# Attention scores in full-array or quarter-array matmuls: changing how one fused attention and gated-MLP kernel makes its scores

## Chip, cores and metric

The kernel runs on one core of one Trainium2 chip. The metric is the device time of one execution in microseconds (us); the median over the runs is compared.

## The reference, cut to what is computed

`q`, `k`, `v` are float32 of shape (8 batches, 8 heads, 576 tokens, 64); `w_in` is (512, 2048), `w_out` (2048, 512). Keys and values are first averaged over groups of 8 tokens, so that each head has 72 keys.

```python
k_p = k.reshape(B, H, Sp, pool, D).mean(axis=3)          # Sp = 72, D = 64
v_p = v.reshape(B, H, Sp, pool, D).mean(axis=3)
scores = scale * np.matmul(q, k_p.transpose(0, 1, 3, 2))
scores = scores - np.max(scores, axis=-1, keepdims=True)
attn = np.exp(scores)
attn = attn / (np.sum(attn, axis=-1, keepdims=True) + 1e-09)
out = np.matmul(attn, v_p)                                # then heads side by side: x (4608, 512)
h = x @ w_in
g = h * np.clip(h + 3.0, 0.0, 6.0) / 6.0
return g @ w_out
```

## The kernel before, in words

The 4608 tokens are cut into 12 blocks (`BLOCKS`: 512, 256, then ten of 384). Blocks 0 to 3 go through the MLP one by one (`Step`: `h` is x times w_in at line 841, `out` is g times w_out at line 872). The eight others go two by two through `super_block` (products at line 1127, output products at line 1204 in `out_plain` or 1279 in `out_seven`), which saves products by sums of quarters of the matrices and streams its weights from DRAM in tiles `ws`. Almost all products are split in high and low fp32r parts; the scores and the transposes are plain float32.

Attention runs ahead of the MLP and in its gaps. Its work for a block is a list of steps (`block_steps`), and `Paced` deals the steps out over slots between groups of MLP matmuls: attention of block 2 and half of block 3 goes beside the MLP of block 1, and so on; attention for a pair of blocks goes beside the super block ahead of it, 0.85 of it (`CUTS`) beside its first products. A block has tiles of 128 tokens (three for a block of 384). Heads are kept as four pairs: `qt` holds a tile's queries as (2 heads x 64 dimensions) on 128 partitions, and `kbds` holds the pooled keys of a pair as a block diagonal, 128 x 144, with zeros off the diagonal. A group `g` is two pairs, four heads.

For one tile and group, `Scores` does the following:

- `product` (line 465): one matmul for each of the two pairs, the full 128 x 128 array, 144 columns. A tile whose 128 tokens lie in two batches (every batch boundary that falls inside a tile; from block 2 on these are the tiles at tokens 1664, 2816 and 3968) needs two per pair, added up, with the other batch's queries set to zero by a memset on POOL (line 241).
- `top` (line 469): DVE takes the maximum of each head.
- `exps` (line 474): four activations on ScalarE (ACT), each with its sum.
- `invert` (lines 491, 492) on DVE, and `divide` (lines 503, 509) on POOL from block 2 on: the main 64 columns of each head go to `a`, the last eight of each head to `ar`.

`transposes` (lines 574, 576) then turns `a` and `ar` on TensorE, ACT and DVE copy them out as high and low parts, and `av` (line 648) multiplies by the values. In `block_steps` a transpose of a group follows three (later two) score steps behind its own. PSUM banks for all this come from `att_bank`, which goes round a list of three (`a0`, `a1`, `o3`), or two while output products run.

The engines' instruction order comes from the Tile framework, apart from a window near the start, in which `ORDER` lists every engine's order by number. `plan` places the loads and preparation of keys and values of a later batch: the first `SIDE` steps ahead of their first use.

## Time and profile before

| | us |
|---|---|
| median of 3 runs | 886.65 (886.44 to 888.14) |
| the profiled execution's own time | 887.28 |
| its span, first to last instruction | 885.5 |
| PE (TensorE matmul) busy in it | 868.3 (98%) |
| DVE busy | 650.5 (73%) |
| ACT busy | 551.9 (62%) |
| POOL busy | 81.4 (9%) |

PE are matmul records, PEld the loads of stationary operands (LDWEIGHTS), DVE is VectorE, ACT ScalarE, POOL GpSimd, SP the queue that issues most DMAs. A float32 matmul of the program shows as two MATMUL records, each with its own LDWEIGHTS; a transpose and an fp32r matmul show as one. A record's duration reaches from its start to a modelled end, and successive matmuls overlap; the pace of matmuls is therefore read from the distance between starts.

### The profile page before, as it was taken

The numbers are of one execution on the slowest core, as the hardware profiler recorded it, in microseconds if no ns is written. First come the engines' busy times: TensorE is split into PE (matmuls) and PEld (weight loads), VectorE is DVE, ScalarE is ACT, GpSimd is POOL, SyncE is SP. The second block draws the span as 40 slices with busy tenths as digits, with TensorE's granted clock in tenths as the row PEclk, the third lists the DMA queues.
The fourth block names the chain that finished last, engine by engine and source line by source line (L and its number), as shares of the span: only waits on it lengthen the run. The fifth ranks groups of instructions, "written<-read, shape, count | busy, mean of one in ns | idle before, by whom it ended". The sixth has DMA issues, their size and how long they took to land.

```text
span 885.5 us, 15623 instructions
## 1 busy us (share of the span) xinstructions
PE 868.3 (98%) x5360; PEld 812.0 (92%) x5360; DVE 650.5 (73%) x1322; ACT 551.9 (62%) x1515; POOL 81.4 (9%) x168
## 2 busy tenths in 40 slices
PE   7999999999999999999999999999999999999998
PEld 7788888988989999999888999899999999999998
DVE  5887754567877885878888588987588887466664
ACT  6998766655666654887444688655576756354442
POOL 4100002110111100112000101100110200000000
PEclk9999999999999999999999999999999999999999
DMA  9970206995425254996697969877886687877784
GB/s 315 391 280 0 77 20 202 366 318 161 122 80 161 60 156 123 367 308 214 205 284 234 379 217 288 247 258 246 277 302 219 202 270 243 275 256 239 268 268 134
DMA packets 124654, 200.00 MB, mean 226 GB/s; under 512 B 13216, under 2 KB 81056, under 8 KB 124576
## 3 DMA queue, kind: packets, MB, share of 16 engines
q1 hardware_dynamic: 124432, 199.00, 68.7%
q8 instruction: 43, 0.70, 0.3%
q14 instruction: 35, 0.29, 0.1%
q10 hardware_dynamic: 144, 0.00, 0.0%
HBM read 158.08 MB, written 40.89 MB: 225 GB/s over the span
## 4 chain that ended last, share of the span: by engine, by line
PE 80%; DVE 7%; DMA 7%; ACT 3%; SPq 1%; issue 1%; DVEq 0%; ACTq 0%
PE psx L1127 21%; PE psx L1279 20%; PE pso L872 12%; PE psh L841 12%; PE psx L1204 7%; PE psa L648 4%; PE psa L465 3%; DMA wsFalse<-wd 2%; DMA stage<-q_l 2%; ACT e L474 2%; PE psa L574 1%; DMA wd<-wq 1%; DMA qt<-q_l 1%; DMA wsTrue<-wd 1%; DVE vst L385 1%
## 5 line engine op out<-in xcount | busy, mean ns | idle before, releaser
L1127 PE MATMUL psx<-x,wsFalse 128*128 128x384 f32 x768 | 150.8, 339 | 1.2 <-DMA wsFalse<-wd 1.2
L841 PE MATMUL psh<-xhi,w 128*128 128x384 f32 (+2 forms) x520 | 146.2, 340 | 0.1
L1127 PEld LDWEIGHTS psx<-x,wsFalse 128*128 128x128 f32 x768 | 132.7, 188 | 2.3 <-ACT part L1113 1.2
L1113 ACT CAST part<-g 128x768 fp32r<-128x768 f32 x100 | 83.3, 837 | 75.1 <-PE psx L1279 56.0
L872 PE MATMUL pso<-w,ghi 128*128 128x512 f32 x384 | 120.6, 399 | 0.4 <-ACT o L877 0.4
L1115 DVE TENSOR_TENSOR part<-g,part 128x768 fp32r<-128x768 f32 x100 | 95.1, 955 | 35.1 <-ACT part L1113 34.8
L1127 PE MATMUL psx<-x,wsTrue 128*128 128x384 f32 x576 | 116.1, 340 | 0.1
L1279 PE MATMUL psx<-wsFalse,part 128*128 128x256 f32 x864 | 109.6, 283 | 0.8 <-DVE g L1098 0.4
L1279 PEld LDWEIGHTS psx<-wsFalse,part 128*128 128x128 f32 x864 | 106.4, 190 | 1.6 <-ACT kept L1254 1.0
L1127 PEld LDWEIGHTS psx<-x,wsTrue 128*128 128x128 f32 x576 | 99.6, 188 | 0.8 <-DVE g L1092 0.4
L841 PEld LDWEIGHTS psh<-xhi,w 128*128 128x128 f32 x520 | 93.3, 188 | 7.5 <-DVE g L853 0.4
L474 ACT ACTIVATE e<-psa,mx 128x72 f32<-128x72 f32 x256 | 78.7, 324 | 31.4 <-DVE mx L469 29.7
L841 PE MATMUL psh<-xlo,w 128*128 128x384 f32 (+2 forms) x260 | 87.1, 336 | 0.0
L503 POOL TENSOR_TENSOR a<-e,sm 128x256 f32<-128x256 f32 x60 | 40.2, 671 | 504.4 <-DVE sm L492 414.8
L1279 PE MATMUL psx<-wsTrue,part 128*128 128x256 f32 x648 | 82.1, 283 | 0.0
L1279 PEld LDWEIGHTS psx<-wsTrue,part 128*128 128x128 f32 x648 | 79.6, 190 | 0.0
L1090 ACT ACTIVATE r<-g,small 128x384 f32<-128x384 f32 x96 | 58.5, 622 | 33.6 <-DVE g L1098 33.0
L872 PEld LDWEIGHTS pso<-w,ghi 128*128 128x128 f32 x384 | 68.9, 188 | 11.0 <-ACT o L877 0.7
L872 PE MATMUL pso<-w,glo 128*128 128x512 f32 x192 | 74.6, 399 | 0.0
L1098 DVE TENSOR_TENSOR g<-psx,c 128x384 f32<-128x384 f32 x96 | 52.0, 552 | 28.7 <-PE psx L1127 23.1
L1092 DVE SCALAR_TENSOR_TENSOR g<-r,g 128x384 f32<-128x384 f32 x96 | 54.6, 579 | 14.0 <-ACT r L1090 13.5
L1107 ACT COPY c<-psx 128x384 f32<-128x384 f32 x96 | 44.9, 485 | 23.8 <-PE psx L1127 23.7
(139 smaller groups left out, 1453.9 us busy)
## 6 DMA issues: line engine op xcount, KB each, us to landing
wsFalse<-wd SPq DMA_DIRECT2D x64, 512.0 KB, 4.8
wsTrue<-wd SPq DMA_DIRECT2D x48, 512.0 KB, 4.9
wsFalse<-w2d SPq DMA_DIRECT2D x31, 512.0 KB, 5.0
wsFalse<-w2t SPq DMA_DIRECT2D x27, 512.0 KB, 5.3
wsTrue<-w2d SPq DMA_DIRECT2D x21, 512.0 KB, 5.1
wsTrue<-w2t SPq DMA_DIRECT2D x21, 512.0 KB, 5.3
raw<-w_in_l SPq DMA_DIRECT2D x16, 512.0 KB, 8.4
raw<-w_out_l SPq DMA_DIRECT2D x16, 512.0 KB, 8.9
```

The lines of the kernel that those rows point to most:

```text
L474: nc.scalar.activation(self.e[:, h], self.ps[:, h], AF.Exp, bias=self.mx[:, h : h + 1], accum_out=self.sm[:, h : h + 1])
L841: nc.tensor.matmul(self.ps, l[f][:, c, :], r[:, c, :], start=c == 0 and i == 0, stop=c == NCC - 1 and i == 2)
L872: nc.tensor.matmul(pos, l, r, start=f == 0 and i == 0, stop=f == NF - 1 and i == 2)
L1090: nc.scalar.activation(r, src, AF.Relu, bias=half_low, scale=GSCALE / (6.0 * WSCALE))
L1092: nc.vector.scalar_tensor_tensor(out=g_of[i][:, k], in0=r, scalar=GSCALE, in1=src, op0=ALU.min, op1=ALU.mult)
L1098: nc.vector.tensor_tensor(out=g_of[i][:, k], in0=ps, in1=kept, op=ALU.add)
L1107: nc.scalar.copy(c, ps)
L1113: nc.scalar.copy(t[:, 0], src)
L1115: nc.vector.tensor_tensor(out=t[:, 1], in0=src, in1=t[:, 0].bitcast(F32), op=ALU.subtract)
L1127: nc.tensor.matmul(ps, w[:, l, c * P : (c + 1) * P], t[:, r, c], start=o in (1, 2, 5) and c == 0 and k == 0, stop=c == 1 and k == 2, skip_ ...
L1204: nc.tensor.matmul(to, l, w[:, qs, r], start=f == 0 and k == 0, stop=end and k == 2)
L1279: nc.tensor.matmul(to, t[:, l, k, i * P : (i + 1) * P], w[:, k, r], start=begin and k == 0 and y == 0 and i % 2 == 0, stop=m == NM - 1 and ...
```

## The change

From block 2 on, `TileScores` takes the place of `Scores`. For each pair of heads it issues four matmuls instead of one: head `r` of the pair lies on 64 of the partitions, and a half of the tile's tokens makes 64 columns of the stationary operand, so that each matmul uses a 64 x 64 quarter of the array, with 72 columns moving. The two heads of a pair go to different PSUM banks, the two token halves to different partitions of them. A tile's 16 matmuls stand together in program order. Since each half tile is a product of its own, a tile across two batches needs no second product and no zeros. The maxima are two instructions for a tile, as before; the exponentials come in two steps of four; add and reciprocal come once for all eight heads; the division writes in place, the tail first, so that the tile `a` is gone and `e` holds all eight heads.

The steps of a tile are now product, first exponentials, second exponentials with the division; the transposes of both groups of the tile before come behind these three, the last tile's at the block's end behind an empty step. `SIDE` goes from 12 to 16 and the preparation of values ends two steps earlier. Blocks 0 and 1 keep `Scores`; their two-batch tile writes each half's partitions alone. `ORDER` is numbered anew for the window's changed instructions (TensorE 600 to 610, DVE 186 to 181, ACT 214 to 210, POOL 25 to 21, SP 61 to 59).

```diff
-SIDE = 12
+SIDE = 16
...
     def load_q(tile):
         qtiles[tile] = []
+        t = pool.tile([P, NPAIR, P], F32, name="qt", bufs=2)
         for i, (b, s0, n, _) in enumerate(tile):
-            t = pool.tile([P, NPAIR, P], F32, name="qt", bufs=2) if i == 0 else ring("qt")
-            t = t if i == 0 else t[:, : NPAIR * P].rearrange("p (c t) -> p c t", c=NPAIR)
-            if n < P:
-                nc.gpsimd.memset(t[:, :, P // 2 :] if i == 0 else t[:, :, : P // 2], 0.0)
-            nc.sync.dma_start(t[:, :, i * (P // 2) : i * (P // 2) + n], q[b, :, :, s0 : s0 + n])
+            mine = t[:, :, i * (P // 2) : i * (P // 2) + n]
+            nc.sync.dma_start(mine, q[b, :, :, s0 : s0 + n])
             after_mark()
-            qtiles[tile].append(t)
+            qtiles[tile].append(mine)
...
         def product(self):      # Scores, blocks 0 and 1
             ps = att_bank()
-            last = len(self.tile) - 1
...
-                for r, (qt, (b, _, _, _)) in enumerate(zip(qtiles[self.tile], self.tile)):
-                    nc.tensor.matmul(to, qt[:, p, :], kbds[b % 2][:, p, :], start=r == 0, stop=r == last)
+                for r, (qt, (b, _, n, _)) in enumerate(zip(qtiles[self.tile], self.tile)):
+                    nc.tensor.matmul(
+                        to[r * (P // 2) : r * (P // 2) + n], qt[:, p, :], kbds[b % 2][:, p, :], start=True, stop=True
+                    )
...
+    class TileScores:
+        def product(self):
+            tile = self.tile
+            banks = att_bank(), att_bank()
+            self.mx, self.sm = (pool.tile([P, NG, 4], F32, name=f"{m}s", bufs=2) for m in ("mx", "sm"))
+            halves = [slice(x * D, (x + 1) * D) for x in range(2)]
+            before = last_pe() if len(window) == 2 else None
+            for p in range(NPAIR):
+                for r in (1, 0):
+                    for x, half in enumerate(halves):
+                        part = x % len(tile)
+                        b = tile[part][0]
+                        nc.tensor.matmul(
+                            banks[r][half, p * SP : (p + 1) * SP],
+                            qtiles[tile][part][halves[r], p, half if len(tile) == 1 else slice(0, D)],
+                            kbds[b % 2][halves[r], p, r * SP : (r + 1) * SP],
+                            start=True,
+                            stop=True,
+                        )
+                        if before:
+                            behind(traced[-1], before)
+                        before = traced[-1].name
+            self.ps = [x[:, : NPAIR * SP].rearrange("p (n s) -> p n s", s=SP) for x in banks]
+            self.e = pool.tile([P, NG, 4, SP], F32, name="e", bufs=2)
...
+            for r in (1, 0):
+                to = self.mx.rearrange("p g (i r) -> p (g i) r", r=2)[:, :, r]
+                nc.vector.tensor_reduce(out=to, in_=self.ps[r], axis=AX.X, op=ALU.max, negate=True)
...
+        def exps(self, g):
+            for h in range(4):
+                nc.scalar.activation(
+                    self.e[:, g, h],
+                    self.ps[h % 2][:, 2 * g + h // 2],
+                    AF.Exp,
+                    bias=self.mx[:, g, h : h + 1],
+                    accum_out=self.sm[:, g, h : h + 1],
+                )
...
+        def finish(self, engine):
+            e, sm = self.e, self.sm
+            nc.vector.tensor_scalar(out=sm, in0=sm, scalar1=1e-9, scalar2=None, op0=ALU.add)
+            nc.vector.reciprocal(sm, sm)
+            rest = rests[self.tile] = pool.tile([P, NG, 2 * REM], F32, name="ar", bufs=2)
+            for g in range(NG):
+                to = e[:, g].rearrange("p h s -> p (h s)")[:, : 4 * D]
+                engine.tensor_tensor(
+                    out=rest[:, g].rearrange("p (c h s) -> p c h s", c=2, h=4),
+                    in0=e[:, g, None, :, D:].broadcast_to([P, 2, 4, SR]),
+                    in1=sm[:, g, None, :, None].broadcast_to([P, 2, 4, SR]),
+                    op=ALU.mult,
+                )
+                engine.tensor_tensor(
+                    out=to.rearrange("p (h s) -> p h s", h=4),
+                    in0=e[:, g, :, :D],
+                    in1=sm[:, g, :, None].broadcast_to([P, 4, D]),
+                    op=ALU.mult,
+                )
+                attn[self.tile, g] = to
...
-        for t in tiles_of[j]:
+        for n, t in enumerate(tiles_of[j] if j > 1 else ()):
+            x, by = TileScores(t), nc.gpsimd
+            steps.append((loads_behind(t), x.product, "scores", [b for b, *_ in t]))
+            steps.append(([], lambda x=x: x.exps(0), None, ()))
+            steps.append(([], lambda x=x, by=by: (x.exps(1), x.finish(by)), None, ()))
+            while todo:
+                turn()
+            todo.extend((t, g) for g in range(NG))
+        if j > 1:
+            steps.append(([], None, None, ()))
+
+        for t in tiles_of[j] if j < 2 else ():
...
-                side_steps(b), ("scores", "av"), (begin - SIDE, begin), (begin, uses("av", b)[0])
+                side_steps(b), ("scores", "av"), (begin - SIDE, begin), (begin - 2, uses("av", b)[0])
```

## Rows read from the trace of the kernel before

**Rows 1.** The profile's page: busy time, share of the span and instructions of TensorE; the clock granted to it in 40 slices, in tenths; the chain of work that ended last, by engine.

```profile
PE 868.3 (98%) x5360; PEld 812.0 (92%) x5360; DVE 650.5 (73%) x1322; ACT 551.9 (62%) x1515; POOL 81.4 (9%) x168
...
PEclk9999999999999999999999999999999999999999
...
PE 80%; DVE 7%; DMA 7%; ACT 3%; SPq 1%; issue 1%; DVEq 0%; ACTq 0%
```

**Rows 2.** Groups of instructions by line, engine and operation with shapes apart: count, busy us and mean ns of one, then the engine's idle time before them.

```profile
L1279 PE MATMUL psx<-wsFalse,part 128*128 128x256 f32 x864 | 109.6, 283 | 0.8 <-DVE g L1098 0.4 <-ACT kept L1254 0.4
...
L474 ACT ACTIVATE e<-psa,mx 128x72 f32<-128x72 f32 x256 | 78.7, 324 | 31.4 <-DVE mx L469 29.7 <-POOL a L503 1.1 <-POOL ar L509 0.6
...
L465 PE MATMUL psa<-kbd,qt 128*128 128x144 f32 x288 | 45.8, 287 | 0.5 <-DVE arem L600 0.3
...
L503 POOL TENSOR_TENSOR a<-e,sm 128x256 f32<-128x256 f32 x60 | 40.2, 671 | 504.4 <-DVE sm L492 414.8 <-ACT r L1090 24.2 <-ACT wq L945 17.3
...
L509 POOL TENSOR_TENSOR ar<-e,sm 128x64 f32<-128x64 f32 x60 | 23.4, 389 | 4.8 <-PE pso L872 4.1 <-DVE sm L492 0.7
...
L491 DVE TENSOR_SCALAR sm<-sm 128x4 f32<-128x4 f32 x72 | 14.0, 198 | 23.7 <-ACT e L474 19.6 <-POOL a L503 2.5 <-ACT stage L474 1.0
...
L492 DVE RECIPROCAL sm<-sm 128x4 f32<-128x4 f32 x72 | 12.6, 176 | 1.7 <-DVE sm L491 0.2
```

**Rows 3.** The score matmuls (line 465) alone in five stretches of the span: length, PE busy (records), PEld busy (records), granted clock, DMA share, GB/s.

```profile
0.00:55.00 55.00, 8.44 (x56) 7.63 (x56) 1.00 0.96 345
55.00:150.00 95.00, 3.75 (x24) 3.46 (x24) 1.00 0.24 80
150.00:345.00 195.00, 14.48 (x92) 13.37 (x92) 1.00 0.57 176
345.00:567.00 222.00, 14.88 (x92) 13.44 (x92) 1.00 0.82 271
567.00:700.00 133.00, 8.88 (x56) 8.12 (x56) 0.99 0.79 255
```

**Rows 4.** PE in order of time, merged: start us, time from the first start to the last end, what, how many records. First products of a super block and behind them a group of a tile across two batches, then output products, then a group of a tile in one batch.

```profile
635.84 1.21 PE L1127 MATMUL psx<-x,wsTrue 128*128 128x384 f32 x6
636.88 1.14 PE L465 MATMUL psa<-kbd,qt 128*128 128x144 f32 x8
...
694.40 1.46 PE L1279 MATMUL psx<-wsFalse,part 128*128 128x256 f32 x11
...
699.60 0.65 PE L465 MATMUL psa<-kbd,qt 128*128 128x144 f32 x4
```

**Rows 5.** PE in order of time near 98 us: the only matmuls of 64 moving columns, float32, each record with a 128-column stationary operand of its own.

```profile
97.71 0.33 PE L648 MATMUL psa<-a,v 128*128 128x64 f32 x2
97.87 0.39 PE L648 MATMUL psa<-a,vrem 96*128 96x64 f32 x2
98.09 0.39 PE L574 MATMUL psa<-ident,a 128*128 128x128 f32 x2
```

**Rows 6.** PE in order of time: the first matmul behind a stretch of no work, and the next one of its kind.

```profile
196.29 0.44 PE L648 MATMUL psa<-ahi,vhi 128*128 128x384 f32 x1 [0.25 <-DVE alo L587]
196.57 0.34 PE L648 MATMUL psa<-alo,vhi 128*128 128x384 f32 x1
```

**Rows 7.** What PE waited for, us in total, times, longest.

```profile
PE psa L574 <- POOL a L503: 2.1, 2, 1.4
...
PE psx L1127 <- DMA wsFalse<-wd: 1.2, 2, 0.9
```

**Rows 8.** PE in order of time from 189.5 us, beside the MLP of block 2.

```profile
189.55 0.65 PE L465 MATMUL psa<-kbd,qt 128*128 128x144 f32 x4
...
190.74 0.34 PE L841 MATMUL psh<-xhi,w 128*128 128x384 f32 x1
191.26 0.41 PE L574 MATMUL psa<-ident,a 128*128 128x128 f32 x2 [0.19 <-issue]
191.51 0.27 PE L576 MATMUL psa<-ident,ar 128*128 128x128 f32 x1
192.49 0.44 PE L574 MATMUL psa<-ident,a 128*128 128x128 f32 x2 [0.71 <-POOL a L503]
```

**Rows 9.** POOL in order of time at the same place.

```profile
190.27 0.31 POOL L241 MEMSET qt<- 128x256 f32 x1 [10.87 <-PE psa L465]
191.82 0.61 POOL L503 TENSOR_TENSOR a<-e,sm 128x256 f32<-128x256 f32 x1 [1.24 <-DVE sm L492]
```

**Rows 10.** Two stretches around 566 us: length, busy us (count) of PE, PEld, DVE, ACT and POOL, granted TensorE clock (1.00 is 2.4 GHz), DMA share, GB/s.

```profile
564.00:567.40 3.40, 1.59 (x9) 0.98 (x8) 3.28 (x10) 1.41 (x4) 0.91 (x2) 0.98 0.78 257
567.40:570.80 3.40, 3.40 (x18) 3.40 (x17) 3.28 (x9) 2.81 (x7) 0.00 (x0) 0.51 0.92 301
```

**Rows 11.** ACT in order of time: the first of eight exponentials in a row, and the reading of the sum behind the last.

```profile
395.09 0.32 ACT L474 ACTIVATE e<-psa,mx 128x72 f32<-128x72 f32 x1 [0.57 <-DVE mx L469]
...
397.37 0.24 ACT L474 ACTIVATION_READ_ACCUMULATOR e<-psa,mx 128x1 f32 x1
```

**Rows 12.** Three longer stretches (beside the MLP of block 2, beside the first and the second super block's products), columns as in rows 10.

```profile
180.00:262.00 82.00, 79.57 (x432) 71.17 (x431) 61.64 (x168) 47.33 (x163) 9.82 (x20) 1.00 0.55 165
...
345.00:433.00 88.00, 86.76 (x504) 82.37 (x503) 69.09 (x169) 64.31 (x214) 14.13 (x28) 1.00 0.80 264
...
492.00:567.00 75.00, 73.10 (x451) 71.89 (x449) 59.77 (x138) 55.98 (x189) 13.05 (x27) 1.00 0.83 277
```

More of the change, by code (lines that the diff above doesn't have):

```diff
@@ L85 @@
         154 151 149 155 157 160 156 152 166 158 161 159 167 170-172 162-163 168 164 173 165 174 176 178 169
-        175 183 177 180-181 179 187 186 184 188 185 194-197 189 202-205 198-199 182 200 208-211 190-191 201
-        206 192 207 212-213 193
+        175 183 177 180-181 179 187 186 184 188 185 189 198-201 194-195 182 196 204-207 190-191 197 202 192
+        203 208-209 193
     """,
     "Pool": """
-        0-1 12 2-3 18 4 7-8 10 5 9 6 14 13 16 15 17 11 19-20 24 21 23 22
+        0-1 12 2-4 7-8 10 5 9 6 14 13 16 15 11 17-20
     """,
@@ L93 @@
         2-3 1 0 4-5 8 6-7 14 9 11 10 22-24 21 20 13 12 15 18 16 19 25-26 28 31 17 27 32 34 33 29 41 30 44 51
-        35 48 46 43 36 47 39 52 59 42 37-38 45 40 50 49 53-55 57-58 60 56
+        35 48 46 43 36 47 39 52 59 42 37-38 45 40 50 49 53-55 57-58 56
     """,
@@ L439, in pool_second @@
         place_rest(1, rest[:, :, :D])
+    exps_of = {}
     class Scores:
@@ L452, in __init__ @@
             else:
-                self.e = pool.tile([P, 4, SP], F32, name="e", bufs=2)
+                if g == 0:
+                    exps_of[tile] = pool.tile([P, NG, 4, SP], F32, name="e", bufs=2)
+                self.e = exps_of[tile][:, g]
                 self.a = None
@@ L497, in divide @@
             if self.a is None:
-                self.a = pool.tile([P, 4 * D], F32, name="a", bufs=3)
                 if self.g == 0:
@@ L501, in divide @@
                 self.rest = rests[self.tile][:, self.g]
+                self.a = e.rearrange("p h s -> p (h s)")
             copies = 3 if self.first else 2
-            engine.tensor_tensor(
-                out=self.a[:, : 4 * D].rearrange("p (h s) -> p h s", h=4),
-                in0=e[:, :, :D],
-                in1=sm[:, :, None].broadcast_to([P, 4, D]),
-                op=ALU.mult,
-            )
-            engine.tensor_tensor(
-                out=self.rest.rearrange("p (c h s) -> p c h s", c=copies, h=4),
-                in0=e[:, None, :, D:].broadcast_to([P, copies, 4, SR]),
-                in1=sm[:, None, :, None].broadcast_to([P, copies, 4, SR]),
-                op=ALU.mult,
-            )
@@ L515, in divide @@
-            attn[self.tile, self.g] = self.a
+            main = self.a[:, : 4 * D].rearrange("p (h s) -> p h s", h=4), e[:, :, :D], sm[:, :, None].broadcast_to([P, 4, D])
+            rest = (
+                self.rest.rearrange("p (c h s) -> p c h s", c=copies, h=4),
+                e[:, None, :, D:].broadcast_to([P, copies, 4, SR]),
+                sm[:, None, :, None].broadcast_to([P, copies, 4, SR]),
+            )
+            for to, x, y in (main, rest) if self.first else (rest, main):
+                engine.tensor_tensor(out=to, in0=x, in1=y, op=ALU.mult)
@@ new lines, in divide, with last_pe, __init__ @@
+            attn[self.tile, self.g] = self.a
+    def last_pe():
+        return next(i for i in reversed(traced) if i.engine == mybir.EngineType.PE).name
+    class TileScores:
+        def __init__(self, tile):
+            self.tile = tile
+        def product(self):
[21 more added lines that the diff above has]
+            self.e = pool.tile([P, NG, 4, SP], F32, name="e", bufs=2)
+            self.later = after_mark if late else no_slot
+            for r in (1, 0):
+                to = self.mx.rearrange("p g (i r) -> p (g i) r", r=2)[:, :, r]
+                nc.vector.tensor_reduce(out=to, in_=self.ps[r], axis=AX.X, op=ALU.max, negate=True)
+                self.later()
+        def exps(self, g):
[7 more added lines that the diff above has]
+                )
+                self.later()
+        def finish(self, engine):
[18 more added lines that the diff above has]
+                attn[self.tile, g] = to
```

14 lines of the change are left out of this document (6 added, 8 removed).

## The prediction, made before the changed kernel was run

> **What bounds the kernel now.** I read the page's busy shares first, then the granted clock, the chain, the groups and the waits. TensorE is busy for 98% of the span, at the full 2.4 GHz in nearly every slice, and holds four fifths of the chain that ended last [rows 1]. All it waited for longer than a moment is a handful of places of about 1 us [rows 7]. DVE and ACT have a quarter and more of each long stretch free [rows 12], and POOL is at 9%. So the time is the sum of what TensorE's instructions take one behind the other. The reader should not add up the mean durations: an output product lasts 283 ns [rows 2], but eleven of them fill 1.46 us [rows 4], so that (1.46 - 0.283) / 10 = 0.118 us lie between starts and 0.165 us of each duration is a tail over which the next one runs. What counts for the change is the distance between starts of the score matmuls, not their 287 ns.
>
> **What it removes.** The score records from block 2 on: the stretch to 55 us holds those of blocks 0 and 1; behind it are 24 + 92 + 92 + 56 = 264 [rows 3]. That agrees with the code: 30 tiles at 4 matmuls and 3 of them at 8 make 132, two records each. Their pace: eight in 1.14 us [rows 4], (1.14 - 0.287) / 7 = 0.122 us for 144 columns. Removed: 264 x 0.122 = **32.2 us**, 0.98 us for a tile in one batch, 1.95 us for one across two.
>
> **What it adds.** 30 tiles x 16 matmuls x 2 records = 960 records of 72 columns; at half the columns 0.061 us each. The trace has no record on a part of the array, so what four quarters do beside each other is bounded from both sides: four abreast 960 x 0.061 / 4 = 14.6 us; two abreast 29.3; none beside another 58.6 us, which is 26 us more than is removed. There is a second bound, from the loads of the stationary operand. The only 64-column matmuls of the trace, four records between 97.71 and 98.09 us, are 0.095 us apart [rows 5], although 64 columns at the pace above are 0.054 us: there the load of 128 stationary columns sets the pace, at about 0.10 us. Half as many stationary columns are about 0.05 us, an estimate from these rows, and a tile now has 32 loads: one at a time they would be 1.6 us for a tile, 48 us in all; two abreast 24, four abreast 12. I take four abreast for both, **+14.6 us**: a pair's two heads lie on different partitions and write different banks, and its two token halves use different columns of the array and write different partitions, so no two of the four share a quarter or an output. Rows do not prove it; they leave it open, and the ends are kept.
>
> **Changing the array's division.** Sixteen quarter matmuls stand between full ones, so the array changes over twice a tile, 60 times. No row shows it. At the least it is free. At the most, the next instruction waits for the last one's tail, 0.165 us, and then for its own load, which else is hidden: the first matmul behind an idle stretch takes 0.44 us and its neighbour 0.34 [rows 6], so 0.10 us more. That is 60 x 0.265 = 15.9 us. I take the tail alone, 60 x 0.165 = **+9.9 us**, since the load of a quarter is half as long and partly beside the tail.
>
> The Trainium skill (TensorEngine Tiling (Array Packing), Tiling Modes, Key Properties) says that a change of tiling mode drains TensorE, and that quarters otherwise work independently, loads and matmuls alike. No run here shows it yet; by the rule the sum keeps the 9.9 us, and without any drain it would be 868.1 us.
>
> **Stalls.** TensorE stood for transposes that waited for POOL's division twice, 2.1 us by the list [rows 7]: once near 192 us, 0.71 us [rows 8], where POOL had stood in front of a memset of `qt` until 190.27 us and came to the division only at 191.82 [rows 9]; and once at 564 us, where PE is busy 1.59 of 3.40 us, followed by 3.40 us at a granted clock of 0.51, 1.2 GHz [rows 10]. The second costs about 1.8 us of standing and 3.40 x 0.49 = 1.7 us of half speed. The change takes the memsets away (0.31 us of POOL each) and puts four steps between a tile's division and its transposes. What is late next is the second group's transposes, which take a bank that the next tile's scores held, and so wait for its eight exponentials: these are 2.3 us of ACT (395.09 to 397.37 [rows 11]), 1.2 us for the last four. Beside the first super block's products go 0.85 of the 44 steps of two blocks, 37; the 54 paced products of six matmuls, each (1.21 - 0.34) / 5 = 0.174 us [rows 4, 6], are 56 us alone, so there are at least 1.5 us to a step, and two steps pass between. That covers 1.2 us with an ACT instruction ahead of it. Both old stalls are where a stage ends and steps come close together, though, and those places stay. Ends: both gone, 0.7 + 1.8 + 1.7 = -4.2 us; two more like them, +4.2. I take **-1.0 us**.
>
> **Edits at nothing.** The maxima, 240 exponentials and POOL's 120 products are as many as before. Add and reciprocal come 30 times instead of 60: 30 x (198 + 176) ns = 11 us less on DVE [rows 2], which has at least 15 us free in each stretch [rows 12], so TensorE gains nothing. On POOL the four divisions of a tile now stand together, 2 x (671 + 389) ns = 2.1 us, behind ACT's last exponential; the four steps, 6 us and more, cover them; without cover the second group's transposes would wait 1.1 us. Query loads keep their number and their place before a tile's first step; on SP they are still queued among the weight loads, and a buffer now comes free a few steps earlier. Key loads go 16 steps ahead instead of 12, but a block has 4 more steps, so in time they are where they were; value preparation ends two steps, some 3 us, earlier. DMA engines are at 0.80 to 0.83 beside the super blocks [rows 12]; with 1% less TensorE time that is no bound, and the waits for weights, 1.2 us [rows 7], can at most double.
>
> **The sum** on the profiled execution: 887.28 - 32.2 + 14.6 + 9.9 - 1.0 = 878.6 us. Its own time lies 0.6 us above the median of the runs, so **878.0 us** for the median.
>
> **The rivals.**
>
> *Two abreast.* The two records of one matmul lie on the same quarter. If TensorE starts its records strictly in order, the second holds up the next matmul until the first has gone through, and only the second and the next one's first run beside each other: a matmul per 0.061 us, 29.3 us in all, a full tile again 0.98 us. Sum 887.28 - 32.2 + 29.3 + 9.9 - 1.0 = 893.3, on the median 892.6: slower. It is slower only from a price of 0.13 us a tile for the changes of division on (3.9 us that are left, over 30); with none it would be 882.8. For it: every record shown starts behind the one before it, at full pace. Against it: none of those had a free quarter beside it.
>
> The Trainium skill (TensorE: Matmul & The Clock Gate, Part 3, The mechanism) reports that matmuls start and end strictly in program order; no row here has quarters to test that, and by it this rival would be the likelier.
>
> *Loads one behind another.* 48 us in place of 14.6: 887.28 - 32.2 + 48 + 9.9 - 1.0 = 912.0, on the median 911.4. For it: the 64-column rows are bound by the load [rows 5]. Against it: those loads all went to the same whole array.
>
> *Waits for banks.* Four abreast, but where steps bunch (the 12 tiles of blocks 2 to 5, which are dealt out beside the shorter blocks) TensorE stands for the last four exponentials, 1.2 us each: 878.0 + 14.4 = 892.4. It decides from steps closer than 0.6 us. The few stalls of the kernel before speak against it; that product and exponentials now hold two of three banks speaks for it.
>
> *Nothing comes of it:* four abreast, and changes of division at their full price with a stall or two: 878.0 + 6.0 + 4 = 888.
>
> **Chances.** A change under 0.2%, 1.8 us, is about what a measurement of this kernel cannot tell from none. Four abreast 0.52, of which 0.46 faster, 0.04 the same, 0.02 slower (the last case above); its own range is 866 to 886. Two abreast 0.29: 0.09 faster (division nearly free), 0.05 the same, 0.15 slower. Loads one by one 0.12, slower. Waits for banks 0.07: 0.01 the same, 0.06 slower. Together faster 0.55, same 0.10, slower 0.35. The range 866 to 902 takes in the first two and the waits, and leaves out loads one by one (0.12) and some 0.05 at its ends.
>
> **What would show it.** In the profile after: 5360 - 264 + 960 = 6056 PE records. On the new line, starts of a tile's 32 records: all within 0.5 us is four abreast, 1.0 two, 1.6 to 2.0 one. The distance from the last full matmul to the first quarter, and back, beyond 0.12 us is the price of the change of division. DVE's add and reciprocal 30 fewer, no POOL memset of `qt`. The stalls at 192 and 564 us gone or not, and the clock there. The forecast is wrong if a tile's scores with both changes take over 0.98 us, or if transposes or products wait for ACT or POOL more than the 2.1 us of before.

## The result and the profile after

The changed kernel takes **893.66 us** (median of 5 runs, 890.71 to 895.61) against 886.59 us for the kernel before on the same chip: a ratio of 1.0074, 95% interval 1.0049 to 1.0098. It is slower; the forecast was faster, 878.0 us.

The page after, in the lines that answer to [rows 1]:

```profile
PE 865.1 (97%) x6056; PEld 797.2 (89%) x6056; DVE 641.1 (72%) x1262; ACT 550.3 (62%) x1515; POOL 80.2 (9%) x160
...
PEclk9999999999999999999999999999999999999999
...
PE 77%; DMA 8%; DVE 7%; ACT 5%; issue 1%; SPq 1%; DVEq 0%; ACTq 0%
```

TensorE has the 6056 records that were forecast and is busy 3.2 us less, yet the span grew from 885.5 to 893.0 us. The groups of the new lines (count and mean ns; [rows 2, 3]):

```profile
L534 PE MATMUL psa<-kbd,qt 64*64 64x72 f32 x960 | 22.6, 229 | 0.1
...
L565 DVE TENSOR_SCALAR sms<-sms 128x8 f32<-128x8 f32 x30 | 5.1, 169 | 25.8 <-ACT e L554 25.7
```

One tile's scores in order of time (PE, merged; start us, time to the last end):

```profile
291.62 0.60 PE L919 MATMUL psh<-xhi,w 128*128 128x384 f32 x2
292.15 0.73 PE L534 MATMUL psa<-kbd,qt 64*64 64x72 f32 x32
292.81 0.44 PE L919 MATMUL psh<-xlo,w 128*128 128x384 f32 x1
```

and the starts of its records, us:

```
292.147 292.153 292.160 292.167 | 292.260 292.267 292.273 292.280 | 292.323 ... | 292.635 292.642 292.648 292.655
```

Four start 7 ns apart, the next four 62 ns after them, 32 within 0.51 us: **four abreast**. The loads of the quarters do the same, four of them 7 ns apart.

To see where the time went I added up the distances between starts of TensorE's records by kind; what a distance has over the usual one of its kind (more than 0.06 us over) is called standing, and what the places beside a tile's quarters have over it is the change of division. In us:

| profiled run | MLP products | scores | changes of division | other attention | standing |
|---|---|---|---|---|---|
| before | 747.7 | 39.2 | 0 | 73.2 | 18.9 |
| after | 750.4 | 20.0 | 11.0 | 70.6 | 33.6 |

By the table the scores with their changes of division fell by 8.2 us. That is too much: its 20.0 us are 30 tiles at 0.50 us and 40 full records at 0.122. The two-batch tile of block 1 isn't among them; its 16 records (line 464) now have 64 stationary columns, start two at a time 7 ns apart, and take 0.84 us for a group where it was 0.98. These 1.7 us stand in the other columns. Read tile by tile, by how far the matmuls behind are pushed back, the quarters with both changes take 0.86 us where the full array took 0.98; over the 30 tiles that is 6.4 us less.

The MLP products, as many as before, take 2.7 us more, and standing grew by 14.7 us: 4.6 in the first 24 us (other attention there fell by 2.4; that start varies with the first loads, and a second profiled run of the same kernel stood 2.6 us there, less than before's 3.2), 2.3 from there to 303 us (up to 1.7 of them the tile of block 1), 7.8 between 343 and 435 us, and 0.1 behind. What PE waited for ([rows 7] of before):

```profile
PE psx L1205 <- DVE g L1176: 3.4, 2, 2.9
...
PE pso L950 <- ACT o L955: 1.8, 2, 1.2
PE psx L1205 <- DMA wsTrue<-wd: 1.8, 1, 1.8
...
PE psx L1282 <- DVE g L1170: 1.4, 1, 1.4
PE psa L641 <- POOL e L576: 1.1, 1, 1.1
```

The two longest waits, 2.9 and 1.8 us, stand at the border to the super blocks. PE there, in order of time:

```profile
348.32 3.74 PE L1205 MATMUL psx<-x,wsFalse 128*128 128x384 f32 x20
354.93 2.36 PE L1205 MATMUL psx<-x,wsFalse 128*128 128x384 f32 x12 [2.86 <-DVE g L1176]
357.22 0.73 PE L534 MATMUL psa<-kbd,qt 64*64 64x72 f32 x32
359.75 1.56 PE L1205 MATMUL psx<-x,wsTrue 128*128 128x384 f32 x6 [1.81 <-DMA wsTrue<-wd]
```

and the same place by stretches, columns as in [rows 10]:

```profile
351.00:357.00 6.00, 3.14 (x19) 2.78 (x17) 1.21 (x3) 3.62 (x19) 0.00 (x0) 1.00 0.88 254
357.00:360.60 3.60, 1.79 (x39) 1.43 (x38) 2.75 (x8) 2.78 (x14) 2.42 (x4) 1.00 0.96 356
360.60:364.10 3.50, 3.50 (x13) 3.50 (x12) 0.79 (x4) 2.32 (x10) 0.00 (x0) 0.51 1.11 264
```

TensorE stands, and a few microseconds later it gets 1.2 GHz for 3.5 us, another 1.7 us lost. In the kernel before, TensorE is busy through all of 351 to 364 us at 2.4 GHz, with DMA engines already at a share of 1.01 to 1.10:

```profile
351.00:357.00 6.00, 6.00 (x37) 5.69 (x36) 4.26 (x12) 4.20 (x20) 0.86 (x2) 1.00 1.01 347
357.00:360.60 3.60, 3.60 (x24) 3.60 (x22) 1.14 (x4) 2.70 (x10) 1.73 (x4) 1.00 1.10 273
360.60:364.10 3.50, 3.50 (x23) 3.33 (x23) 3.50 (x9) 2.88 (x8) 0.00 (x0) 1.00 1.05 397
```

In all, 1.2 GHz took as much from both profiled runs: before has its 3.4 us at 567 us [rows 10], where after runs at 2.4 GHz.

What DVE waits for at the border (in order of time):

```profile
346.15 0.76 DVE L1017 TENSOR_TENSOR wq<-w 128x256 f32<-128x256 f32 x2 [4.03 <-DMA wd<-wq]
346.95 1.27 DVE L1022 TENSOR_TENSOR wq<-wq 128x128 f32<-128x128 f32 x4
348.95 0.69 DVE L1024 TENSOR_TENSOR wq<-wq 128x512 fp32r<-128x512 f32 x1 [0.73 <-ACT wq L1023]
349.56 0.81 DVE L549 TENSOR_REDUCE mxs<-psa 128x4 f32<-128x288 f32 x2
354.32 0.56 DVE L1176 TENSOR_TENSOR g<-psx,c 128x384 f32<-128x384 f32 x1 [3.95 <-DMA wd<-wq]
```

These `wq` lines are a piece of the kernel that the prediction never mentions. Beside blocks 2 and 3, `sums_of` prepares the super blocks' weights in sixteen rounds: six sums on DVE, a cast on ACT, a subtraction on DVE, four stores to DRAM, from where `ws` is loaded. All rounds use one buffer, so the next begins when the stores of the last have landed. From 227 us on, a round starts 3.5 to 5.1 us behind the end of the one before it, with a single longer pause of 7.1 us; in the kernel before it is 3.5 to 4.2 us and one of 10.4. The sixteenth ends at 347.6 us before and at 349.6 after, though TensorE was 0.8 us ahead of before's course at 334 us. The 2 us between them are not the point: in a second profiled run of the changed kernel, whose start was not late, it ended at 347.7 us, and TensorE stood 3.0 us all the same, since it got there earlier by as much. The first gate's tile lies in the memory of that buffer, and the first weights are what was stored.

### The profile page after: what moved, and what is told of

Its sections match the earlier page's. It is cut to its first block, busy times and chain, and to the rows that moved or that the text cites. A ratio compares the mean times of both kernels' runs of the same rounds, so it can differ in the third digit from the quotient of the medians.

```text
span 893.0 us, 16773 instructions
## 1 busy us (share of the span) xinstructions
PE 865.1 (97%) x6056; PEld 797.2 (89%) x6056; DVE 641.1 (72%) x1262; ACT 550.3 (62%) x1515; POOL 80.2 (9%) x160
## 4 chain that ended last, share of the span: by engine, by line
PE 77%; DMA 8%; DVE 7%; ACT 5%; issue 1%; SPq 1%; DVEq 0%; ACTq 0%
PE psx L1205 22%; PE psx L1357 20%; PE pso L950 11%; PE psh L919 11%; PE psx L1282 7%; PE psa L715 3%; ACT e L554 2%; PE psa L534 1%; PE psa L641 1%; DMA raw<-w_out_l 1%; DMA qt<-q_l 1%; DMA raw<-w_in_l 1%; DMA vst<-v_l 1%; DMA wd<-wq 1%; DVE g L1170 1%
## 5 line engine op out<-in xcount | busy, mean ns | idle before, releaser
L554 ACT ACTIVATE e<-psa,mxs 128x72 f32<-128x72 f32 x240 | 73.3, 330 | 13.9 <-DVE mxs L549 13.8
L570 POOL TENSOR_TENSOR ar<-e,sms 128x64 f32<-128x64 f32 x60 | 22.4, 392 | 543.0 <-DVE sms L566 409.9
```

The lines of the kernel that those rows point to most:

```text
L554: nc.scalar.activation(self.e[:, g, h], self.ps[h % 2][:, 2 * g + h // 2], AF.Exp, bias=self.mx[:, g, h : h + 1], accum_out=self.sm[:, g, ...
```

## The experiments

Ratios are to the kernel before, measured beside each of them, with 95% intervals. The framework orders every engine's instructions anew when the program changes: pad640, g6_first and before384 keep the order of the kernel they come from, the others don't, so that some of what they gain or lose is the new order.

### Memory and pace

The changed kernel's attention tiles take 640 bytes less, so that the weight slots `ws` begin at 65856 instead of 66496. Two kernels move only that: pad640 adds 640 unused bytes to the changed kernel, before384 adds 384 to the kernel before (66880, the same place modulo 1024 as after).

```diff
-            self.mx, self.sm = (pool.tile([P, NG, 4], F32, name=f"{m}s", bufs=2) for m in ("mx", "sm"))
+            self.mx, self.sm = (
+                pool.tile([P, 48], F32, name=f"{m}s", bufs=2)[:, :8].rearrange("p (g h) -> p g h", g=NG) for m in ("mx", "sm"))
```

> The changed kernel with 640 bytes of each partition left unused behind the attention tiles, so that the streamed weights lie at the same SBUF addresses as before the change (66496 instead of 65856); the order of instructions on all five engines is the changed kernel's. Theory (the slower pace of the output products, 120.7 instead of 119.2 ns from start to start, comes from where their operands lie): the pace in the stretch of the second output products returns to about 119 ns, and the time falls by about 2.5 us, to 891. Rival (the pace comes from what runs beside it): pace stays 120.7 ns, time 893 to 894.

> The kernel before, instruction for instruction, with 384 bytes of unused memory ahead of the weight slots of the feed-forward, so that these lie at the same place modulo 1024 bytes as in the changed kernel. Theory (the pace of the 256-column output products, 119 ns a start before and 121 after, comes from where their operands lie, and repeats every 1024 bytes): 121 ns, and 889 to 890 us, a ratio of 1.003. Rival (it comes from what runs beside them in the changed kernel): 119 ns and no change.

Both theories' pace came true. before384: 890.79 us, **1.0022** [1.0010, 1.0035]. pad640: 888.72 us, **1.0013** [0.9995, 1.0031]. PE in 50 us of the last stage, where output products prevail, the kernel before, before384 and then pad640 (in brackets: records):

```profile
824.65:874.65 50.00, 50.00 (x419) 1.00 0.75 250
```

```profile
827.38:877.38 50.00, 50.00 (x413) 1.00 0.74 251
```

```profile
824.33:874.33 50.00, 50.00 (x418) 1.00 0.74 251
```

The changed kernel has 413 in such a stretch, as before384. By starts the 256-column products come every 119.4 ns with the slots at 66496 and every 121.1 ns at 65856 or 66880, and the MLP products take 747.6 us in pad640, 750.4 in before384. So 2.7 us of the loss have nothing to do with attention. Why the address matters is open.

The changed kernel and pad640 were run again, beside the kernels that follow:

> The changed kernel once more, as it is, beside the three kernels below. Both theories: 893 to 895 us, a ratio of about 1.007 to the kernel before; the stall of about 3 us at the border to the super blocks (near 350 us) and the half clock some microseconds behind it should be there again. If the stall is 3 us and the half clock is absent, then the half clock is chance, and about 1.7 us of the loss goes with it.

> The changed kernel with the pad of 640 bytes once more, beside the three kernels below. Both theories: 888 to 889 us, no measurable difference from the kernel before, since what TensorE saves on the scores (39.2 us before, 31.0 with the changes of division) comes back as 8 us more of standing.

after_control: 891.84 us, 1.0041 [1.0026, 1.0055], with the stall of 3.2 us near 350 us and 3.4 us at 1.2 GHz from 352.3 us on, as expected; in time it came out lower than the 893 to 895 us expected. pad_control: 890.52 us, 1.0029 [1.0014, 1.0044], a little worse than pad640: with the pad the changed kernel is level with the kernel before or up to 0.4% slower. The profiled runs of pad640 and pad_control are one program, with spans of 885.9 and 893.0 us. The same two places in both, pad_control first:

```profile
350.00:356.00 6.00, 2.75 (x16) 2.43 (x15) 0.61 (x2) 3.46 (x18) 0.00 (x0) 1.00 0.85 241
356.00:362.80 6.80, 6.08 (x48) 5.43 (x47) 3.75 (x9) 5.19 (x24) 2.00 (x4) 0.50 1.04 308
...
424.40:427.80 3.40, 3.40 (x9) 2.68 (x10) 2.81 (x8) 1.08 (x4) 0.88 (x2) 0.52 0.37 127
```

```profile
347.00:353.00 6.00, 3.26 (x19) 2.94 (x18) 0.94 (x2) 3.79 (x20) 0.00 (x0) 1.00 0.95 273
353.00:361.00 8.00, 6.75 (x68) 6.32 (x67) 5.87 (x15) 6.75 (x25) 4.56 (x8) 1.00 1.04 358
```

With 2.75 us of work in the 6 us at the border, 6.8 us at 1.2 GHz followed, and 3.4 more near 424 us; with 3.26 us of work, none. Each has one more stretch of 3.4 us, near 571 and 565 us, so that pad_control has 10.2 us more at 1.2 GHz in all; half of that is 5.1 of the 7.1 us between the two. A stall of 3 us can thus bring 1.7 to 3.4 us more with it.

### Quarters or the full array, in the same steps

```diff
-                for r in (1, 0):
-                    for x, half in enumerate(halves):
...
+                to = banks[p // 2][:, p % 2 * 2 * SP : (p % 2 + 1) * 2 * SP]
+                for x in range(len(tile)):
+                    b, n = tile[x][0], tile[x][2]
+                    nc.tensor.matmul(to[x * (P // 2) : x * (P // 2) + n], qtiles[tile][x][:, p, :], kbds[b % 2][:, p, :], start=True, stop=True)
```

full_array is without the pad, pad_full with it:

> The changed kernel with its steps, tiles, in-place division and placements, but with the scores of a tile made by full-array matmuls again, one for each pair (two of 64 stationary columns where a tile lies in two batches), groups in banks instead of heads. Theory (the quarters give 6.5 us and the steps around them lose 13): a tile's scores take 0.98 us, and the time is 893.7 + 6.5 = 900, in any case above 896. Rival (the quarters and the changes of division lose the time): 886 to 888, as before the change.

> The changed kernel's steps and the pad of 640 bytes, with the scores on the full array again (two matmuls of 144 columns a pair in a tile of two batches, one otherwise, 4 or 8 a tile). Beside the kernel with the pad alone (888.7 us, scores 20.0 us and changes of division 11.0 us) it tells what the quarters are worth in steps and memory that are otherwise the same. Theory (TensorE's own work decides, 35.5 us for 31.0): 4 to 5 us slower, 892 to 893 us. Rival (what the quarters save is given back in waits at the same two borders, since the rounds of sums there end by DVE's time and not by TensorE's): 888 to 890 us.

full_array: 890.16 us, 1.0023 [1.0000, 1.0047]. pad_full: 888.10 us, **0.9994** [0.9974, 1.0014]. On TensorE the scores are 35.4 us on the full array and 31.0 in quarters with their changes of division, a gain of 4.4; in time pad_full is level with pad640 or ahead. pad_full's rival holds: TensorE's own work did not decide. Of full_array neither expectation came true: 900 us was 10 too much, so the steps around the scores do not lose 13 us by themselves.

### Earlier loads of keys

```diff
-SIDE = 16
+SIDE = 12
...
-                side_steps(b), ("scores", "av"), (begin - SIDE, begin), (begin - 2, uses("av", b)[0])
+                side_steps(b), ("scores", "av"), (begin - SIDE, begin), (begin, uses("av", b)[0])
```

> The changed kernel with key loads and value preparation placed as before the change (12 steps ahead, no two steps less); the framework orders all engines anew. Theory (quarters gain 6.5 us, and what is lost is the order of the work around them, which comes out by chance of each placement): the border near 350 us comes out differently, and the time moves by up to 5 us either way, 888 to 898, with the scores' own 0.86 us a tile unchanged. Rival (earlier keys and values are the cause): 887 or less, the border's stall gone.

891.42 us, 1.0039 [1.0020, 1.0057], as after_control. TensorE now stood 3.1 us for a load of `qt`, and the stalls at the border shrank to 0.8, 1.5 and 1.9 us: one traded for others, nothing decided.

### The border

g6_first only puts another late tile on the buffer's memory, so that the gate needn't wait for the stores:

```diff
+    late[1].tile([P, 2, 4, HALF], F32, name="g6")
```

> The changed kernel with the super block's gate tile g6 placed where g0 lay, and g0 behind it; nothing else, same order on every engine. g0 lay on the memory of wq, so its first writer on DVE waits until the last stores of wq have landed. Theory (at the border to the super blocks TensorE stands 2.9 us because of that wait, and loses 1.7 us more by the half clock behind it): the 3 us stall at 352 us is gone or under 1 us, the stall for wsTrue at 358 us stays at about 2 us, and the time falls by 3 to 5 us, to 889 or 890. Rival (something else is late there as well, the products or the loads): the stall only moves to the next product, and the time stays at 893 to 894.

892.93 us, 1.0052 [1.0034, 1.0070]. The rival's time. The stall behind the gate is gone, one for the weights stands in its place, and 6.8 us at 1.2 GHz follow (PE in order of time):

```profile
352.20 0.73 PE L534 MATMUL psa<-kbd,qt 64*64 64x72 f32 x32
357.64 2.29 PE L1205 MATMUL psx<-x,wsTrue 128*128 128x384 f32 x6 [4.71 <-DMA wsTrue<-wd]
```

So the shared memory is not the cause; the gate's tile and the weights are two ways in which TensorE comes to wait for the last round. Next, the rounds were begun earlier: all sixteen (sums_early), every 7/4 steps, or the last eight by one step, as shown (sums_half, full_half on the full array, before_half in the kernel before; all but the last with the pad).

```diff
-        hooks[2 + n // NPR].setdefault(2 * (n % NPR), []).append(step)
+        at = 2 * n - (n >= NPR)
+        hooks[2 + at // NF].setdefault(at % NF, []).append(step)
```

> The changed kernel with the pad of 640 bytes, and the sixteen rounds of sums over the query weights dealt out every 7/4 steps instead of every 2, so that the last round starts 3.75 steps, some 17 us, earlier. Theory (the loss at the border is a queue on DVE: the last round, with its store, ends 2 to 3 us too late for the first product's gate, whose tile lies on the round's memory): the stalls of 2.9 and 1.5 us near 348 and 354 us go, no half clock follows, and the time is 883 to 885 us, below the kernel before. Rival (TensorE simply reaches the border earlier and waits there for weights whose loads are bound by the DMA engines): the stall at 348 us gives way to one of the same 3 to 4 us for wsTrue, and the time stays at 888 to 889 us, that of the kernel with the pad alone.

> The changed kernel with the pad, and only the eight rounds of sums of the last plain block one step earlier (some 4.6 us); the eight rounds before them stay. Theory (the gate of the first super block's first product waits for the store of the last round, and the weights for what was stored): the stalls of 2.7 and 1.2 us at the border near 348 and 354 us go, nothing new comes before 300 us, 884 to 885 us. Rival (whatever is moved on DVE there pushes something else behind it, as when all sixteen rounds were moved: a wait of DVE for a value load, with gates queued behind it): the border is free and another stall of 2 to 3 us stands elsewhere, 887 to 890 us.

> The same move of the last eight rounds, in the kernel with the changed steps, the pad and scores on the full array. Theory (the two border stalls there, 2.5 and 1.8 us, have the same cause): 884 to 885 us, as the kernel with quarters and the same move, or up to 4 us more than that by TensorE's own 35.4 us for 31.0. Rival (the quarters' saving is never paid out, since waits fill what it leaves): not more than 1 us from the kernel with quarters and the same move.

> The same move in the kernel before, which waits at the border for 0.9 us. Theory (the border's stall came with the change, since TensorE arrives 4.5 us earlier there): no gain from it, 887 to 889 us. Rival (the border costs the kernel before as well, in ways that its waits don't show): 885 us or less, and the move is worth as much without the change.

sums_early 894.00 us, 1.0054 [1.0034, 1.0074]; sums_half 894.72 us, 1.0070 [1.0053, 1.0088]; full_half 891.28 us, 1.0034 [1.0017, 1.0051]; before_half 890.09 us, 1.0016 [1.0002, 1.0030]. All four lost time where a gain or none was expected, and the first two more than their rivals allowed; full_half was 3.4 us ahead of sums_half, where 1 us was the most expected. In sums_half the border isn't free: TensorE stands 2.4 us for `wsTrue` near 358 us, with 6.8 us at 1.2 GHz from there on. In full_half it is, but TensorE stands 3.6 us near 274 us (first fence, from PE's waits), also with 6.8 us at 1.2 GHz behind it. In sums_early the border is free too, and TensorE stands 2.8 us near 386 us, where DVE waits for a value load with the gate queued behind it (second fence, DVE in order of time):

```profile
PE psh L918 <- DVE g L930: 4.3, 3, 3.6
```

```profile
386.32 0.69 DVE L381 TENSOR_TENSOR vst<-vst 128x512 f32<-128x512 f32 x1 [2.44 <-DMA vst<-v_l]
386.93 0.55 DVE L1170 SCALAR_TENSOR_TENSOR g<-r,psx 128x384 f32<-128x384 f32 x1
```

And the last round ended at 347.3, 350.2, 349.1 and 350.3 us (346.0 in pad640): an earlier place in the program did not end it earlier, and every round still started 3.5 us or more behind the end of the one before. So the two free borders are no gain of the move: at 340 us full_half was 7.3 us behind pad_full and sums_early 9.2 us behind pad640, and whoever comes late need not wait. Then six of the seven DVE instructions of a round went to POOL, in all three kernels:

```diff
-            nc.vector.tensor_tensor(
+            nc.gpsimd.tensor_tensor(
...
-            nc.vector.tensor_tensor(out=q[:, to], in0=q[:, a], in1=q[:, b], op=how)
+            nc.gpsimd.tensor_tensor(out=q[:, to], in0=q[:, a], in1=q[:, b], op=how)
```

> The changed kernel with the pad, and six of the seven DVE instructions of each round of sums (the two of 256 columns and the four of 128, 96 instructions, 31 us of DVE with 16 us of waiting for the store ahead of them) on POOL instead. Theory (DVE's order is what gives the saving back): the stalls of TensorE for DVE's gates between 200 and 360 us go, the stalls in all fall from 27-34 us to about 20, and the time is 882 to 885 us, below the kernel before. Rival (the weights' transfers are the bound at the border): DVE is free, TensorE waits for wsTrue or wsFalse instead, 887 to 890 us. A second rival: POOL now stands for the stores, the divisions queue behind it, and transposes wait for POOL more than the 1.1 us of now: 888 us or more.

> The same move to POOL with the changed steps, the pad and scores on the full array. Theory (with DVE's queue out of the way TensorE's own work decides, 35.4 us for 31.0): 3 to 5 us slower than the kernel with quarters and the same move, 886 to 889 us. Rival (waits still fill what the quarters save): within 1 us of it.

> The same move to POOL in the kernel before. Theory (the kernel before stands for little between 200 and 360 us, 4 us by its trace): a gain of 0 to 3 us, 885 to 888 us, so that the changed kernel is the faster of the two once the sums are off DVE. Rival (the move is worth as much without the change): 883 us or less, and the change itself still gains nothing.

pool_sums 898.95 us, 1.0121 [1.0102, 1.0140]; full_pool 892.23 us, 1.0047 [1.0031, 1.0063]; before_pool 892.98 us, 1.0054 [1.0034, 1.0074]. The theory that DVE's load is at fault fell, and so did full_pool's that it would be slower than pool_sums; before_pool, of which a gain was expected, lost 0.5%, with transposes waiting 5.0 us for POOL's division. POOL took over the wait (pool_sums, POOL's waits), and the last round ended at 351.4, 348.0 and 347.6 us, not earlier than with DVE. The profiled run of pool_sums also has four stretches of 3.4 us at 1.2 GHz.

```profile
POOL wq L1020 <- DMA wd<-wq: 64.4, 12, 7.4
```

That left the chain itself. wide gives the sums two buffers in turn, the high halves keep one; full_wide does so on the full array, before_wide in the kernel before (there maxima and sums also share a tile, for room). In all three the weight slots lie at the address of before modulo 1024, so that the pad's effect is in them.

```diff
-        t = early_x[-1].tile([P, 2, 4, P], F32, name="wq", bufs=1)
-        hi, q = t[:, 0], t[:, 1]
+        if not wide:
+            wide.append(early_x[-1].tile([P, 3, 4, P], F32, name="wq", bufs=1))
+        t, at_q = wide[0], 1 + h
+        hi, q = t[:, 0], t[:, at_q]
...
-            nc.sync.dma_start(dram_of(i, o)[:, :, half], t[:, :, at])
+            nc.sync.dma_start(dram_of(i, o)[:, :, half], t[:, 0 : at_q + 1 : at_q, at])
```

> The changed kernel, with the sums of a round written into one of two buffers in turn (the high halves keep one), so that a round's first six DVE instructions no longer wait for the store of the round before; the memory for it comes from 384 bytes of an unused scratch area, which also puts the weight slots of the feed-forward back to where they were modulo 1024 bytes (the pad's effect). Theory (the chain of sixteen rounds, each held by the store of the last, sets the border): the last round ends 4 us or more earlier than 346 us, the stalls at the border (2.7 and 1.2 us) go, 883 to 886 us. Rival (the new order of DVE's and ACT's work brings other stalls, as in the three other moves of this work): the rounds end earlier and the border is free, but stalls between 200 and 340 us grow by as much, 888 to 892 us. Second rival (the cast into the one buffer of high halves still waits for the store): rounds end where they were, no change from 888 to 890 us.

> The same two buffers with the changed steps and scores on the full array. Theory (without the chain TensorE's own work decides, 35.4 us for 31.0): 3 to 5 us slower than the kernel with quarters and two buffers. Rival (waits still fill what the quarters save): within 1 us of it, or faster.

> The kernel before with the same two buffers for the sums; the memory comes from an unused scratch area (896 bytes) and from keeping maxima and sums of a group in one tile, and the weight slots of the feed-forward lie as before modulo 1024 bytes. Theory (in the kernel before the chain of rounds ends at 347.6 us, just as TensorE gets to the border, and TensorE stands there for under 1 us; so only the changed kernel is held by it): 886 to 888 us, within 0.2% of the kernel before, and the changed kernel with two buffers (884.1 us) stays ahead of it. Rival (the chain costs the kernel before as much): 883 to 884.5 us, and the change is worth nothing.

wide: **884.06 us**, **0.9959** [0.9946, 0.9973], the fastest kernel of this work. full_wide: 890.52 us, 1.0037 [1.0023, 1.0052]. before_wide: 884.97 us, **0.9974** [0.9960, 0.9987]. In wide the last round ends at 341.8 us, DVE's wait for the stores (16.2 us between 180 and 350 us in pad640) is off its list (ACT's cast waits 6.8 us for them instead), and PE runs through the border. By the starts of the same MLP products its profiled run is 2.1 us behind pad640's at 340 us and 2.1 us ahead at 366; coming late alone could have saved it 2.1 of these 4.2 us at most:

```profile
346.25 0.73 PE L534 MATMUL psa<-kbd,qt 64*64 64x72 f32 x32
346.91 3.76 PE L1209 MATMUL psx<-x,wsFalse 128*128 128x384 f32 x20
350.51 1.20 PE L1209 MATMUL psx<-x,wsTrue 128*128 128x384 f32 x6
351.55 2.24 PE L1209 MATMUL psx<-x,wsFalse 128*128 128x384 f32 x12
```

That is the theory's step, at its time. But the rival of before_wide holds in part as well: the buffer gives the kernel before 2.1 us, and what the change adds on top, 0.9959 against 0.9974, is less than their intervals can tell apart. TensorE's scores are by some 6.4 us shorter in wide; of these some 5 come back even with the border free.

full_wide tells where. It is 6.5 us slower than wide, more than its theory's 3 to 5: here the quarters are paid out, as they were not between pad_full and pad640. And it is 0.6% slower than before_wide, which has the old steps on the same array, although its border is free as well; its profiled run falls 4.5 us behind that of before_wide between 366 and 435 us, where TensorE waits 1.9 us for DVE near 420 us. By these medians the changed steps with their new order lose 5.6 us, nearly what the quarters gain. How much of that is the steps and how much the order that came with them isn't shown: the same two buffers on the full array with the changed steps gave nothing (full_wide 1.0037, pad_full 0.9994).

wide waits 0.8 to 1.3 us each at places spread over the span, mostly where a step of attention now follows too soon on another:

```profile
PE psa L641 <- DVE arem L667: 1.3, 1, 1.3
PE pso L950 <- ACT o L955: 1.2, 2, 1.0
PE psa L534 <- ACT e L554: 1.2, 1, 1.2
PE psa L641 <- POOL e L576: 1.0, 1, 1.0
```

and it has 3.4 us at 1.2 GHz near 562 us, of which before_wide has none. These were not tried one by one; that they are the rest is the reading of one trace, and not shown.

## Why the prediction was wrong

- **Scores, -32.2 + 14.6 = -17.6.** Right: -19.2 us by the table, of which 2.0 are the tile of block 1, so -17.2. The sum left that tile out; it gained 0.3. Four abreast held for matmuls and loads; the rivals with two abreast and with loads one behind another are out. The Trainium skill (TensorE: Matmul & The Clock Gate, Part 3, The mechanism) says that matmuls start and end strictly in program order; the trace agrees for matmuls as wholes, whose first records and then second records start in turn. What the rival made of the rule does not follow: the second record of a matmul begins a round of 62 ns behind its first, and the next three matmuls did not wait for it. (The records don't name their matmul; the signals of completion stand on the second and fourth of a tile's last four, as they do if these are the second records of the last four matmuls.)
- **Changing the array's division, +9.9.** Right: 11.0 us over 30 tiles, 0.37 us a tile instead of 0.33. In the tile shown the last full matmul's columns end near 292.05 us and the first round of quarters begins 62 ns ahead of the second, at 292.20; back it is 0.21 us. The Trainium skill (TensorEngine Tiling (Array Packing), Tiling Modes) says that a change of mode drains TensorE; the trace agrees, with 0.15 us going and 0.21 us back.
- **Stalls, "I take -1.0 us", ends -4.2 to +4.2.** This is the step that failed: +14.7 us in the profiled run, of which about 2 are the varying start and up to 1.7 the tile of block 1, so 11 or more. The wait at the border with its half clock, 6.4 us of it, is alone more than the upper end. It looked only at the stalls that the trace of before shows, and took their small number for slack. Of the two it named, that of 192 us went (pad640 stands 0.7 us between 123 and 206 us where before stood 2.8), and at that of 564 us TensorE still stands, 0.7 us twice, for ACT and DVE now, but at 2.4 GHz. Not seen was a chain that TensorE does not drive: sixteen rounds through one buffer, which end in the kernel before just when TensorE gets to the border. A kernel that is faster ahead of it only waits there, and the wait brought 1.2 GHz with it. A second buffer made the wait go, which gave 4 us at the border by the traces; the rest of the stalls is spread over the changed steps, with causes that are open.
- **The rival "Waits for banks", 892.4 us at 0.07,** came nearest in time, with its kind of wait (TensorE for ACT and POOL behind a tile's scores) at a few places of 1 us, but the largest wait lies elsewhere. The sign it named was there: transposes and products wait for ACT and POOL for more than 2.1 us in all (1.1 for POOL near 232 us, 1.8 for ACT at line 950 alone). "The few stalls of the kernel before speak against it" was the wrong inference: a wait near zero can mean that two chains end together.
- **Edits at nothing.** DVE's 30 adds fewer and POOL's memsets gone, as said. "DMA engines are at 0.80 to 0.83 ...; that is no bound" rested on a mean over 88 us [rows 12]; from 351 to 364 us they were at 1.01 to 1.10 in the kernel before already. What that share costs by itself was not separated from the chain.
- **Not in the sum at all:** tiles left out move the tiles behind them, +2.7 us on products that the change doesn't touch.

By terms: -19.2 + 11.0 + 2.7 + 14.7 - 2.6 (other attention, most of it the start) = +6.6 us of the 7.5 us between the two profiled runs; the rest lies outside TensorE's first to last record.

## What to carry to other kernels

Before a saving on the bound engine is booked, look beside it for chains with a rhythm of their own (one buffer, compute, store, reload), and ask when they end against the time at which the bound engine will now get there; that the trace of before shows no stall doesn't mean that there is slack. Read busy shares at the place where a transfer matters, not over the stage. Hold the addresses of untouched tiles fixed when two versions are compared, and when a move brings the wait to another place each time, shorten the chain instead of shifting it.

## What was not expected of the hardware

- Quarters of 64 x 64: loads and matmuls of four start 7 ns apart, at 62 ns a round for 72 float32 columns; going to quarters cost 0.15 us and back 0.21.
- The pace of 256-column output products depends on where their tiles lie: 119.4 ns a start with the slots at 66496, 121.1 ns at 65856 and 66880; the 384-column products kept theirs.
- One program, two profiled runs: 13.6 us at 1.2 GHz in the one, behind three stalls, and 3.4 us in the other, 5.1 us of time between them. Ahead of the first of these stretches TensorE had worked 2.75 us of 6; at the same place in the other run it had worked 3.26, and kept 2.4 GHz.
